# Giving the small matmuls of a recurrent attention kernel one tile shape each, and evacuating the end of a segment in halves

## The chip, the core and the metric

The kernel runs on one core of a Trainium2 chip. The metric is device time in microseconds, from the start of the program to its end. Five engines matter here: TensorE (in the profile PE for matmuls and PEld for weight loads), VectorE (DVE), ScalarE (ACT), GpSimd (POOL) and SyncE (SP), which issues most DMAs. Each engine works off its own queue in order; semaphores tie the queues together. A matmul takes a stationary operand (the loaded weights, `lhsT`) and a moving operand (`rhs`); a tile shape such as 32*128 or 128*64 in the profile means that the matmul uses so many rows and columns of the array. Results land in PSUM, from where VectorE or ScalarE copy them to SBUF. Such a copy is called an evacuation here.

## The reference

Two attention layers are computed from separate inputs and set side by side in the output. Part A is a sliding local attention; the change does not touch it. Part B is a recurrent attention with memory, and nearly all of the time is spent there:

```python
for s in range(n_seg):                       # 64 segments of 32 tokens
    xs = x[:, s * seg_len:(s + 1) * seg_len, :].copy()
    h = jnp.concatenate([mem, xs], axis=1)   # 8 memory rows + 32 tokens = 40
    q = jnp.einsum('btd,dhe->bhte', h, Wq)   # 640 -> 32 heads of 192
    k = jnp.einsum('btd,dhe->bhte', h, Wk)
    v = jnp.einsum('btd,dhe->bhte', h, Wv)
    scores = jnp.einsum('bhqe,bhke->bhqk', q, k) * scale
    scores = jnp.where(mask[None, None], scores, -1000000000.0)
    p = _softmax(scores, axis=-1)
    o = jnp.einsum('bhqk,bhke->bhqe', p, v)
    o = jnp.einsum('bhte,hed->btd', o, Wo)
    mem = o[:, :M, :].copy()                 # the next segment's memory
    outs.append(o[:, M:, :])
```

The segments form a chain: the first 8 output rows of one are the memory of the next. Matrices are bfloat16.

## The kernel before, in words

Part B works through 64 segments. In each, the 32 heads are taken as 4 groups (`g`) of 8 heads; a group's projection is 8 x 192 = 1536 columns wide. `project32` computes one projection of one group for 32 rows of the input: four matmuls of tile 128*32 stand side by side in the array, so the result `acc` has 128 partitions (4 column blocks of 32 tokens) and 384 columns (two heads of 192). A segment's 40 rows are 32 main rows and 8 late ones. The late rows of four segments are projected together, in 32 rows at once, only when a group is due (`RENEW`), and are kept until their segment comes (in `Lb` buffers for Q and K, in `LV` for V).

For Q and K, `to_sb` evacuates `acc` into `sb`; `turn` transposes the three 128-column chunks of `sb` into the PSUM tile `pt` (partitions = positions within two heads, free = chunk, block, token); `spread` copies it into `QT` or `KT`. The two heads of a block take 384 positions, so chunk 0 belongs to the first head, chunk 2 to the second, and the middle chunk is half and half. `turn_late` does the same for the late rows, into `QT`/`KT` or into `Lb`; POOL copies from `Lb` later (L488).

`scores(g)` computes all 8 heads' scores into one PSUM tile `Sps`: for each head one matmul over a whole chunk (128 rows, tile 128*64) and one over half of the middle chunk (64 rows, tile 64*64). `softmax` is a chain on VectorE and ScalarE; `put_p` writes the normalized result into `P`; `turn_p` transposes `P` with two 128*128 transposes and evacuates it into `PT`. `mix(g)` multiplies `PT` with V: per group 16 matmuls of tile 32*128 (whole chunks) and 16 of tile 32*64 (halves of the middle chunk) into four PSUM tiles `OTps`, which are evacuated into `OT`. `project_out` accumulates `OT` times `Wo` into `Y` with tiles of 128*64.

At the end of a segment `Y` is evacuated into `row` (`Ysb`, L643, one ScalarE copy of 320 columns), `memory_rows` transposes the 8 memory rows into the next segment's input `HX`, and the late Q of one group, which was projected meanwhile, is evacuated into `sb` and turned.

What sets the order: TensorE's order is the order of the calls in `segment`, written out by hand (`manual_schedule` for PE alone). The order on VectorE, ScalarE, POOL and SP is made by the framework's scheduler. `evacuate` alternates between ScalarE and VectorE by a count over all its calls, so that one more or one fewer call moves all later ones to the other engine:

```python
    def evacuate(dst, src):
        copies["n"] += 1
        (nc.scalar.copy if copies["n"] % 2 else nc.vector.tensor_copy)(dst, src)
```

PSUM is held by three pools: 3 buffers for `acc`, 4 for everything small (`ps_x`: `pt`, `Sps`, `OTps`), 1 for `Y`. Weights that do not fit in SBUF are streamed in every segment by SP through 5 slots (`ws`, tile name `t` in the profile, read from `wcopy_k`, `wcopy_v` and `wcopy_o`): 23 units a segment.

Of the kernel before, what the change touches and what calls it, by code (L numbers as in the profile page):

```python
# [271 lines left out]
def part_b(ctx, tc, B_x, B_mem0, B_Wq, B_Wk, B_Wv, B_Wo, out, ident, n_seg, pre, nbuf, mid):  # L272
# [139 lines left out]
    free = [cpool.tile([128, 12, M], BF16, name=f"Lb{i}") for i in range(BLOCKS)]  # L412
# [35 lines left out]
    def to_sb(p):  # L448
        sb = qk_sb.tile([128, 384], BF16, tag="sb", name="sb")
        evacuate(sb[:], p[:])  # L450
        return sb

    def turn(sb):
        pt = ps_x.tile([128, 3, 4, 32], FP32, tag="x")
        for c in range(3):
            nc.tensor.matmul(pt[:, c], lhsT=sb[:, 128 * c:128 * c + 128], rhs=ident, start=True, stop=True)  # L456
        return pt

    def spread(dst, src):
        evacuate(dst.rearrange("p (j c) n -> p c j n", c=3), src)  # L460

    def tokens(t):
        return t[:, 0:12 * L].rearrange("p (a n) -> p a n", n=L)

    def turn_late(sb, m, g, s, start):

        pt = turn(sb)
        T = tokens(QT if m == "q" else KT)
        for t in range(start, next_start(m, g, start)):
            if t == s:  # L470
                dst = T[:, :, 32:L]
            else:
                late[m, g, t] = free.pop(0)
                dst = late[m, g, t][:]
            spread(dst, pt[:, :, :, M * (t % 4):M * (t % 4) + M])

    def project_qk(s, m, g):
        T = QT if m == "q" else KT
        renew = s == 0 or f"{m}{g}" in RENEW[s % 4]
        Xs = [ahead(s), main(s)] if renew else [main(s)]  # L480
        sbs = [to_sb(p) for p in project32(Xs, m, g)]

        def turns():
            if renew:
                turn_late(sbs[0], m, g, s, s)
            else:
                b = late.pop((m, g, s))
                nc.gpsimd.tensor_copy(tokens(T)[:, :, 32:L], b[:])  # L488
                free.append(b)
            pt = turn(sbs[-1])  # L490
            spread(tokens(T)[:, :, 0:32], pt[:])

        return turns

    def values(s, g):
        renew = s == 0 or f"v{g}" in RENEW[s % 4]
        ps = project32([ahead(s), main(s)] if renew else [main(s)], "v", g)
        if renew:
            evacuate(LV[g][:], ps[0][:])
        Vst = one.tile([128, 384], BF16, tag="Vst")  # L500
        evacuate(Vst[:], ps[-1][:])
        return Vst

    def scores(g):
        KTt = tokens(KT)
        Sps = ps_x.tile([128, 4, L], FP32, tag="x")
        plist = []
        for a in range(4):
            plist += [(False, 0, a, 0, 3 * a, 128), (True, 0, a, 0, 3 * a + 1, 64),
                      (True, 64, a, 1, 3 * a + 1, 128), (False, 0, a, 1, 3 * a + 2, 128)]  # L510
        plist.sort()
        seen = set()
        last = {p[3]: n for n, p in enumerate(plist)}
        for n, (_, lo, a, g2, cc, hi) in enumerate(plist):
            nc.tensor.matmul(Sps[64 * g2:64 * g2 + 64, a, :], lhsT=QT[lo:hi, L * cc:L * cc + 64], rhs=KTt[lo:hi, cc, :],  # L515
                             start=(g2 not in seen), stop=(n == last[g2]), tile_position=(lo, 64 * g2))
            seen.add(g2)
        return Sps

    def softmax(Sps):  # L520
# [19 lines left out]
            nc.vector.tensor_tensor(out=P[:, k, :, at:at + hi - lo], in0=t1[:, :, lo:hi],  # L540
                                    in1=sm[:].unsqueeze(2).to_broadcast([128, 4, hi - lo]), op=ALU.mult)

    def turn_p():

        pt = ps_x.tile([128, 2, 128], BF16, tag="x")
        for late in range(2):
            nc.tensor.transpose(pt[:, late, :], P[:, late].rearrange("p a n -> p (a n)"), ident)  # L547
# [4 lines left out]
    def mix(g, PT, Vst):  # L552

        ps = [ps_x.tile([128, 3, L], FP32, tag="x", name=f"OTps{a}") for a in range(4)]
        for wide in (True, False):
            for late, V in enumerate((Vst, LV[g])):
                for half in range(2):
                    for a in range(4):
                        if wide:
                            dst, e0, e1, col = ps[a][:, 2 * half, :], 256 * half, 256 * half + 128, 0  # L560
                        else:
                            dst, e0, e1 = ps[a][64 * half:64 * half + 64, 1, :], 128 + 64 * half, 192 + 64 * half
                            col = 64 * half
                        nc.tensor.matmul(dst, lhsT=V[32 * a:32 * a + 32, e0:e1], rhs=PT[32 * a:32 * a + 32, late, half, :],  # L564
                                         start=(wide and late == 0 and half == 0), stop=(not wide and late == 1),
                                         tile_position=(32 * a, col))
# [14 lines left out]

    def memory_rows(s, Ysb):
        pt = ps_x.tile([128, 5, M], FP32, tag="x")
        for dc in range(5):
            for gv in range(2):
                c0, c1 = max(128 * dc, 320 * gv), min(128 * dc + 128, 320 * gv + 320)
                if c0 < c1:
                    lo = c0 - 128 * dc
                    nc.tensor.matmul(pt[lo:lo + c1 - c0, dc, :], lhsT=Ysb[:, c0 - 320 * gv:c1 - 320 * gv],
                                     rhs=ident[:, 64 * gv:64 * gv + M], start=True, stop=True,  # L590
                                     tile_position=(0, lo))
        nc.vector.tensor_copy(HXs[(s + 1) % 2][:, :, 0:M], pt[:])

    def segment(s):
        last = s + 1 == n_seg
        load_x(s + 1)
        tq, tk, V, PT = {}, {}, {}, {}
# [10 lines left out]
        V[0] = values(s, 0)  # L608
# [5 lines left out]
        mix(0, PT[0], V[0])  # L614
        V[1] = values(s, 1)
# [7 lines left out]
        mix(1, PT[1], V[1])  # L623
        V[2] = values(s, 2)
# [6 lines left out]
        mix(2, PT[2], V[2])  # L631
        V[3] = values(s, 3)
        project_out(Y, 2, range(0, 4))
        PT[3] = turn_p()
        project_out(Y, 2, range(4, 6))
        mix(3, PT[3], V[3])
# [6 lines left out]
        nc.scalar.copy(Ysb, Y[:])  # L643
# [84 lines left out]
```

## Time and profile before

| | |
|---|---|
| time, median of 3 runs | 2028.95 us (2024.3 to 2034.06) |
| profiled execution, device time | 2024.66 us |
| profiled execution, span of its instructions | 2022.8 us |
| busy: PE / PEld | 1945.4 / 1243.6 us |
| busy: DVE / ACT / POOL | 1128.3 / 725.6 / 193.6 us |
| instructions | 97144, of them 42512 matmuls and as many weight loads |
| granted TensorE clock, mean | 0.994 |
| HBM read and written | 576.85 MB and 18.87 MB, 295 GB/s over the span |

The span is 1.9 us shorter than the device time; what lies around it is small. The profile's rows give a start in microseconds, a length from the first start to the last end of a merged group, and in brackets how long the engine was idle before and what ended that. A matmul's length holds its way through the array, so matmuls that follow each other overlap in the records; what a matmul costs on TensorE is seen from start to start, not from its length.

### The profile page before, as it was taken

What the parts mean: (1) busy time and instruction counts of PE and PEld (TensorE: products, weight loads), DVE (VectorE), ACT (ScalarE), POOL (GpSimd) and SP (SyncE); (2) the same over time, 40 slices, a digit from 0 to 9 for tenths busy, and PEclk for the clock granted to TensorE, in tenths of its full rate; (3) what the DMA queues carried; (4) which work ended last, traced back from release to release, by engine and by line L of the source; (5) the groups of instructions that cost most, each with busy time, mean ns of one, the idle gap of its engine ahead of it and who ended that gap; (6) DMA issues with size and microseconds to landing.
All of it is one profiled execution on the core that took longest, in us unless ns stands there. A gap on an engine that the chain in (4) does not pass through costs nothing.

```text
span 2022.8 us, 97144 instructions
## 1 busy us (share of the span) xinstructions
PE 1945.4 (96%) x42512; PEld 1243.6 (61%) x42512; DVE 1128.3 (56%) x3622; ACT 725.6 (36%) x2126; POOL 193.6 (10%) x674
## 2 busy tenths in 40 slices
PE   7989999999999999999999999999999999999998
PEld 4656666666666666666666666666666665666665
DVE  5875555555555455555555555555555554555554
ACT  3543333333333333333333333333333333333333
POOL 2000000110001101001001001101001001110110
PEclk9999999999999999999999999999999999999999
DMA  9927999999899999999999989999899988989997
GB/s 343 311 76 269 311 300 305 301 302 307 290 305 304 299 288 312 302 304 303 303 299 297 308 292 311 305 303 299 296 298 303 298 304 284 303 293 300 305 302 257
DMA packets 270123, 596.29 MB, mean 295 GB/s; under 512 B 61065, under 2 KB 72841, under 8 KB 269385
## 3 DMA queue, kind: packets, MB, share of 16 engines
q1 hardware_dynamic: 264770, 585.97, 87.9%
q8 instruction: 333, 5.46, 1.1%
q0 software_dynamic: 4928, 4.11, 0.6%
q14 instruction: 92, 0.75, 0.1%
HBM read 576.85 MB, written 18.87 MB: 295 GB/s over the span
## 4 chain that ended last, share of the span: by engine, by line
PE 71%; DMA 19%; DVE 6%; ACT 1%; issue 1%; SPq 1%; POOL 0%; DVEq 0%; POOLq 0%; ACTq 0%
PE acc L443 33%; PE Y L578 18%; DMA t<-wcopy_k 8%; DMA t<-wcopy_o 6%; PE pt L456 6%; PE Sps L515 4%; PE OTps L564 4%; PE pq L95 2%; PE pt L547 2%; DVE sb L423 2%; DMA out_dram<-row 2%; DMA t<-wcopy_v 1%; PE po L161 1%; DMA wcopy_o<-in_B_Wo_dram 1%; PE py L172 1%
## 5 line engine op out<-in xcount | busy, mean ns | idle before, releaser
L443 PEld LDWEIGHTS <-HX 128*32 128x32 bf16 x19380 | 462.7, 96 | 274.3 <-issue 46.5
L578 PEld LDWEIGHTS <-OT 128*64 128x64 bf16 x6144 | 316.8, 109 | 131.0 <-ACT OT L423 20.0
L578 PE MATMUL Y<-wres_o,OT 128*64 128x320 bf16 x3584 | 344.3, 302 | 2.2
L443 PE MATMUL acc<-wres_q,HX 128*32 128x384 bf16 x6460 | 332.6, 328 | 0.5 <-ACT sb L423 0.2
L443 PE MATMUL acc<-t,HX 128*32 128x384 bf16 x4200 | 309.1, 328 | 12.9 <-DMA t<-wcopy_k 10.1
L578 PE MATMUL Y<-t,OT 128*64 128x320 bf16 x2560 | 277.7, 303 | 10.0 <-DMA t<-wcopy_o 9.2
L423 DVE CAST sb<-acc 128x384 bf16<-128x384 f32 x322 | 178.8, 556 | 186.6 <-PE acc L443 171.3
L443 PE MATMUL acc<-wres_v,HX 128*32 128x384 bf16 x4844 | 276.5, 328 | 0.1
L528 ACT ACTIVATE t<-t 128x160 f32<-128x160 f32 x256 | 86.1, 336 | 439.4 <-DVE t L527 439.4
L443 PE MATMUL acc<-wres_k,HX 128*32 128x384 bf16 x3876 | 224.8, 327 | 0.3 <-issue 0.3
L522 DVE SCALAR_TENSOR_TENSOR t<-Sps,mask 128x160 f32<-128x160 f32 x256 | 82.8, 323 | 214.6 <-PE Sps L515 186.6
L423 ACT CAST sb<-acc 128x384 bf16<-128x384 f32 x324 | 153.6, 474 | 125.1 <-PE acc L443 123.5
L456 PE MATMUL pt<-ident,sb 128*128 128x128 bf16 x1938 | 179.4, 221 | 6.9 <-DVE sb L423 1.7
L423 DVE CAST OT<-OTps 128x120 bf16<-128x120 f32 x512 | 125.5, 271 | 97.4 <-PE OTps L564 96.8
L488 POOL COPY QT<-Lb 128x96 bf16<-128x96 bf16 x252 | 67.4, 267 | 1112.0 <-PE Sps L515 955.2
L456 PEld LDWEIGHTS <-sb 128*128 128x128 bf16 x1938 | 110.2, 97 | 82.3 <-issue 32.3
L515 PEld LDWEIGHTS <-QT 128*64 128x64 bf16 (+1 forms) x4096 | 118.9, 109 | 55.1 <-issue 40.5
L423 ACT CAST OT<-OTps 128x120 bf16<-128x120 f32 x512 | 106.0, 258 | 110.7 <-PE OTps L564 110.4
L515 PE MATMUL Sps<-KT,QT 128*64 128x40 bf16 (+1 forms) x4096 | 137.0, 188 | 2.2 <-DVE KT L423 1.0
L530 DVE TENSOR_REDUCE sm<-t 128x4 f32<-128x160 f32 x256 | 81.8, 320 | 78.7 <-ACT t L528 78.7
L564 PEld LDWEIGHTS <-Vst 32*128 32x128 bf16 (+1 forms) x4096 | 62.2, 97 | 82.3 <-issue 60.5
L564 PE MATMUL OTps<-PT,Vst 32*128 32x40 bf16 (+1 forms) x4096 | 109.7, 192 | 0.0
(75 smaller groups left out, 1916.0 us busy)
## 6 DMA issues: line engine op xcount, KB each, us to landing
t<-wcopy_o SPq DMA_DIRECT2D x640, 320.0 KB, 4.3
t<-wcopy_k SPq DMA_DIRECT2D x512, 384.0 KB, 4.8
t<-wcopy_v SPq DMA_DIRECT2D x320, 384.0 KB, 4.8
wres_q<-in_B_Wq_dram SPq DMA_DIRECT2D x20, 384.0 KB, 7.7
wres_v<-in_B_Wv_dram SPq DMA_DIRECT2D x15, 384.0 KB, 7.8
wres_k<-in_B_Wk_dram SPq DMA_DIRECT2D x12, 384.0 KB, 7.7
wres_o<-in_B_Wo_dram SPq DMA_DIRECT2D x14, 320.0 KB, 6.7
wcopy_o<-in_B_Wo_dram SPq DMA_DIRECT2D x10, 320.0 KB, 8.1
```

The source lines that it names most:

```text
L95: nc.tensor.matmul(pq[32 * d:32 * d + 32], lhsT=wcol[:, k, t, 4 * c + d, :], rhs=xTs[s][:, k, :], start=(k == 0), stop=(k == 4), tile_posi ...
L423: (nc.scalar.copy if copies["n"] % 2 else nc.vector.tensor_copy)(dst, src)
L443: nc.tensor.matmul(ps[n][32 * j:32 * j + 32, :], lhsT=X[:, dc, :], rhs=w[:, 384 * j:384 * j + 384], start=(dc == 0), stop=(dc == 4), tile_ ...
L456: nc.tensor.matmul(pt[:, c], lhsT=sb[:, 128 * c:128 * c + 128], rhs=ident, start=True, stop=True)
L488: nc.gpsimd.tensor_copy(tokens(T)[:, :, 32:L], b[:])
L515: nc.tensor.matmul(Sps[64 * g2:64 * g2 + 64, a, :], lhsT=QT[lo:hi, L * cc:L * cc + 64], rhs=KTt[lo:hi, cc, :], start=(g2 not in seen), sto ...
L522: nc.vector.scalar_tensor_tensor(out=t1[:], in0=Sps[:], scalar=scale, in1=mask[:].unsqueeze(1).to_broadcast([128, 4, L]), op0=ALU.mult, op ...
L528: nc.scalar.activation(t1[:], t1[:], ACTF.Exp)
L530: nc.vector.tensor_reduce(out=sm[:], in_=t1[:], axis=AX.X, op=ALU.add)
L547: nc.tensor.transpose(pt[:, late, :], P[:, late].rearrange("p a n -> p (a n)"), ident)
L564: nc.tensor.matmul(dst, lhsT=V[32 * a:32 * a + 32, e0:e1], rhs=PT[32 * a:32 * a + 32, late, half, :], start=(wide and late == 0 and half = ...
L578: nc.tensor.matmul(Y[64 * gv:64 * gv + 64, :], lhsT=OT[:, L * c:L * c + 64], rhs=w[:, n:n + 320], start=(i == 0 and r == 0), stop=(i == 23 ...
```

## The change

All edits are in part B.

- **V with zeros inside.** `Vst` and `LV` grow from 384 to 448 columns, with 64 zero columns between the two heads. Each half of the middle chunk can then be taken as a whole 128-column chunk whose other half is zero. `mix` issues 32 matmuls of tile 32*128, as many as before in all, and none of 32*64.
- **K's middle chunk twice.** `KT` holds four chunks for each block: the first head's, the middle one with its lower half zero, the second head's, and the middle one with its upper half zero. `scores` issues 16 matmuls of tile 128*64, as many as before in all, and none of 64*64. K can no longer be copied from `pt` in one piece: `fill` takes one copy of two chunks (256 columns for the main rows) and two copies of 64 partitions (128 columns each), in place of one copy of 384. The same holds for the late rows, also for POOL's copies from `Lb`.
- **Transposes of the last group's P.** `turn_p(2)` does, for group 3 alone, four matmuls of tile 128*64 against the identity into float32 in place of two transposes of 128*128.
- **End of a segment.** `Y` into `row` and the late Q into `sb` are each copied in two halves, the first by ScalarE and the second by VectorE. `memory_rows` takes its middle chunk, which needs tile 128*64, first.

```diff
-    KT = cpool.tile([128, 12 * L], BF16, name="KT")
+    KT = cpool.tile([128, 4, 4, L], BF16, name="KT")
...
-    LV = [cpool.tile([128, 384], BF16, name=f"Lv{g}") for g in range(GROUPS)]
+    VW = 448
+    LV = [cpool.tile([128, VW], BF16, name=f"Lv{g}") for g in range(GROUPS)]
+    Vst = cpool.tile([128, VW], BF16, name="Vst")
     nc.gpsimd.memset(P[:], 0.0)
+    nc.gpsimd.memset(KT[:], 0.0)
...
+    for t in LV + [Vst]:
+        nc.gpsimd.memset(t[:, 192:256], 0.0)
...
+    def halves(dst, src, n):
+        nc.scalar.copy(dst[:, 0:n], src[:, 0:n])
+        nc.vector.tensor_copy(dst[:, n:], src[:, n:])
...
+    def fill(copy, m, n0, n1, src):
+
+        if m == "q":
+            copy(tokens(QT)[:, :, :, n0:n1].rearrange("p j c n -> p c j n"), src)
+            return
+        copy(KT[:, :, 0:3:2, n0:n1].rearrange("p j c n -> p c j n"), src[:, 0:3:2])
+        copy(KT[0:64, :, 1, n0:n1], src[0:64, 1])
+        copy(KT[64:128, :, 3, n0:n1], src[64:128, 1])
...
+        for n in range(8):
+            a, part = n // 2, n % 2
+            for g2 in range(2):
+                at = L * (3 * a + g2 + part)
+                nc.tensor.matmul(Sps[64 * g2:64 * g2 + 64, a, :], lhsT=QT[:, at:at + 64],
+                                 rhs=KT[:, a, ((0, 1), (3, 2))[g2][part], :], start=(n == 0), stop=(n == 7),
+                                 tile_position=(0, 64 * g2))
...
+            for h in range(2):
+                nc.tensor.matmul(pt[64 * h:64 * h + 64, late, :], lhsT=src[:, 64 * h:64 * h + 64], rhs=ident,
+                                 start=True, stop=True, tile_position=(0, 64 * h))
...
+        plan = [(late, half, k, col) for late in range(2) for half in range(2)
+                for k, col in (((0, 0), (1, 128)), ((2, 320), (1, 192)))[half]]
+        for n, (late, half, k, col) in enumerate(plan):
+            V = LV[g] if late else Vst
+            for a in range(4):
+                nc.tensor.matmul(ps[a][:, k, :], lhsT=V[32 * a:32 * a + 32, col:col + 128],
+                                 rhs=PT[32 * a:32 * a + 32, late, half, :],
+                                 start=(n == 0), stop=(n == len(plan) - 1), tile_position=(32 * a, 0))
...
-        for dc in range(5):
+        for dc in (2, 0, 1, 3, 4):
...
-        PT[3] = turn_p()
+        PT[3] = turn_p(2)
...
-        nc.scalar.copy(Ysb, Y[:])
+        halves(Ysb, Y[:], 160)
         if not last:
             project32([ahead(s + 1)], "q", gl, range(3, 5), ql)
-            sb = to_sb(ql[0])
+            sb = qk_sb.tile([128, 384], BF16, tag="sb", name="sb")
+            halves(sb[:], ql[0][:], 192)
```

More of the change, by code (lines that the diff above doesn't have):

```diff
@@ L497, in values @@
         ps = project32([ahead(s), main(s)] if renew else [main(s)], "v", g)
[L498 to L502, printed above, removed]
+        for t, p in ((LV[g], ps[0]), (Vst, ps[-1]))[0 if renew else 1:]:
+            v = t[:].rearrange("p (n e) -> p n e", e=64)
+            w = bass.AP(v.tensor, v.offset, [v.ap[0], [256, 2], [1, 192]])
+            evacuate(w, p[:].rearrange("p (h e) -> p h e", h=2))
     def scores(g):
-        KTt = tokens(KT)
         Sps = ps_x.tile([128, 4, L], FP32, tag="x")
[L507 to L517, printed above, removed]
+        for n in range(8):
[5 more added lines that the diff above has]
+                                 tile_position=(0, 64 * g2))
         return Sps
@@ L541, in put_p, with turn_p @@
                                     in1=sm[:].unsqueeze(2).to_broadcast([128, 4, hi - lo]), op=ALU.mult)
-    def turn_p():
-        pt = ps_x.tile([128, 2, 128], BF16, tag="x")
+    def turn_p(split=1):
+        pt = ps_x.tile([128, 2, 128], FP32 if split > 1 else BF16, tag="x")
         for late in range(2):
-            nc.tensor.transpose(pt[:, late, :], P[:, late].rearrange("p a n -> p (a n)"), ident)
+            src = P[:, late].rearrange("p a n -> p (a n)")
+            if split == 1:
+                nc.tensor.transpose(pt[:, late, :], src, ident)
+                continue
+            for h in range(2):
+                nc.tensor.matmul(pt[64 * h:64 * h + 64, late, :], lhsT=src[:, 64 * h:64 * h + 64], rhs=ident,
+                                 start=True, stop=True, tile_position=(0, 64 * h))
         PT = one.tile([128, 2, 2, L], BF16, tag="PT")
@@ L550, in turn_p, with mix @@
         return PT
-    def mix(g, PT, Vst):
+    def mix(g, PT):
         ps = [ps_x.tile([128, 3, L], FP32, tag="x", name=f"OTps{a}") for a in range(4)]
[L555 to L566, printed above, removed]
+        plan = [(late, half, k, col) for late in range(2) for half in range(2)
[6 more added lines that the diff above has]
+                                 start=(n == 0), stop=(n == len(plan) - 1), tile_position=(32 * a, 0))
         for a in range(4):
@@ L607, in segment @@
         tq[2] = project_qk(s, "q", 2)
-        V[0] = values(s, 0)
+        values(s, 0)
         soft = softmax(scores(1))
@@ L613, in segment @@
         tk[2] = project_qk(s, "k", 2)
-        mix(0, PT[0], V[0])
-        V[1] = values(s, 1)
+        mix(0, PT[0])
+        values(s, 1)
         tk[2]()
@@ L622, in segment @@
         tk[3] = project_qk(s, "k", 3)
-        mix(1, PT[1], V[1])
-        V[2] = values(s, 2)
+        mix(1, PT[1])
+        values(s, 2)
         tq[3]()
```

27 lines of the change are left out of this document (11 added, 16 removed).

## The prediction, made before the changed kernel ran

> **What bounds the kernel now.** I read the page's head and its chain first, then a sum over the steady stretch, then the waits, then the timeline around each edit.
>
> ```profile
> span 2022.8 us, 97144 instructions
> ```
> ```profile
> PE 71%; DMA 19%; DVE 6%; ACT 1%; issue 1%; SPq 1%; POOL 0%; DVEq 0%; POOLq 0%; ACTq 0%
> ```
> ```profile
> 200.00:2000.00 1800.00, 1753.56 (x39782) 1122.67 (x39778) 986.25 (x3426) 628.04 (x1920) 176.98 (x629) 1.00 0.92 301
> ```
> ```profile
> PE acc L443 <- DMA t<-wcopy_k: 10.1, 32, 0.9
> ```
>
> In the steady stretch PE is busy for 1753.56 of 1800 us at clock 1.00, and VectorE for 986.25. The DMA share is 0.92, but the longest sum of waits of a matmul for a streamed unit is 10.1 us. So TensorE's order sets the time. A stall in it counts, and so does a saving, until a streamed unit is late.
>
> **Mix.** Four mixes in each of 64 segments. One of them:
>
> ```profile
> 1025.30 0.22 PE L564 MATMUL OTps<-PT,Vst 32*128 32x40 bf16 x8
> 1025.36 0.21 PE L564 MATMUL OTps<-PT,Lv 32*128 32x40 bf16 x8
> 1025.50 0.23 PE L564 MATMUL OTps<-PT,Vst 32*64 32x40 bf16 x8
> 1025.55 0.20 PE L564 MATMUL OTps<-PT,Lv 32*64 32x40 bf16 x8
> 1025.68 0.35 PE L443 MATMUL acc<-wres_v,HX 128*32 128x384 bf16 x4
> ```
> ```profile
> L564 PE MATMUL OTps<-PT,Lv 32*128 32x40 bf16 x2048 | 53.6, 174 | 0.0
> ```
>
> The last wide matmul starts at 1025.36 + 0.21 - 0.174 = 1025.40, the first narrow one at 1025.50: the change of shape costs 0.10 us, in which eight matmuls start elsewhere (0.05 to 0.06). The whole lasts 0.38. Afterwards 32 wide ones take 0.10 for the first sixteen, 0.10 to 0.12 for the others, and 0.11 for the way out (as from narrow: 1025.50 to 1025.68, less 0.07). That is 0.30 to 0.32, so 0.06 to 0.08 saved; I take 0.08, since the second eight started in 0.04. Four: 0.33 a segment.
>
> **Scores.**
>
> ```profile
> 1020.51 0.30 PE L515 MATMUL Sps<-KT,QT 128*64 128x40 bf16 x8
> ```
> ```profile
> 1020.75 0.31 PE L515 MATMUL Sps<-KT,QT 64*64 64x40 bf16 x8
> ```
> ```profile
> 1020.99 0.68 PE L456 MATMUL pt<-ident,sb 128*128 128x128 bf16 x9
> ```
> ```profile
> 1006.61 0.52 PE L515 MATMUL Sps<-KT,QT 128*64 128x40 bf16 x16
> 1007.06 0.46 PE L578 MATMUL Y<-wres_o,OT 128*64 128x320 bf16 x4
> ```
>
> Eight wide ones and the change of shape last 0.24, eight narrow ones and the next change 0.24. Wide ones start in pairs; the last starts at 1020.51 + 0.30 - 0.186 (its length in this window) = 1020.63, so eight take 0.12. Sixteen of one shape take 0.25, plus 0.11 for the way out: 0.36 against 0.48, 0.12 saved in groups 0 to 2. Group 3 stands between matmuls of Y with the same tile 128*64, so both changes go: 0.45 becomes about 0.25, 0.20 saved. Together 0.55 a segment. New is that two pairs running add to the same 40 columns. Matmuls of Y add to the same 320 columns without a gap (four in 0.27 us below), so I take nothing for it; a pair that waited for the whole length of the one before (0.19) would cost 8 x 0.15 a group, the far end.
>
> **Transposes of the last P.**
>
> ```profile
> 1009.61 0.44 PE L578 MATMUL Y<-t,OT 128*64 128x320 bf16 x4
> 1009.88 0.44 PE L578 MATMUL Y<-wres_o,OT 128*64 128x320 bf16 x4
> 1010.25 0.28 PE L547 MATMUL pt<-ident,P 128*128 128x128 bf16 x2
> 1010.47 0.33 PE L578 MATMUL Y<-wres_o,OT 128*64 128x320 bf16 x2
> ```
>
> Y starts a pair every 0.135 us, so its last starts at 1010.02, and Y goes on 0.45 later. With one shape that is 0.135 plus two pairs of 128 columns (0.055 each by the same rate): 0.24, so 0.21 saved. Here a rule can be weighed: two shape changes go, and by the rows each is dear by some 0.1. The Trainium skill, TensorEngine Tiling (Array Packing), Key Properties, says that a change of tiling mode drains the array while a change of tile does not; no price is given there, and the gaps above show about 0.1.
>
> Savings: 0.33 + 0.55 + 0.21 = **1.09 us a segment, 70 us**.
>
> **Copies that take turns.** `fill` copies K from one PSUM tile in three copies, alternating between ScalarE and VectorE, and `halves` splits two evacuations. In the changed order each later copy of such a set waits for a semaphore of the other engine. The trace has this already, in the `Lb` copies from one `pt`:
>
> ```profile
> 1015.71 0.26 DVE L423 CAST Lb<-pt 128x96 bf16<-128x96 f32 x1 [0.25 <-PE pt L456]
> 1016.05 0.24 ACT L423 CAST Lb<-pt 128x96 bf16<-128x96 f32 x1 [0.85 <-DVE Lb L423]
> 1016.39 0.26 DVE L423 CAST Lb<-pt 128x96 bf16<-128x96 f32 x1 [0.43 <-ACT Lb L423]
> ```
> ```profile
> L423 DVE CAST KT<-pt 128x384 bf16<-128x384 f32 x113 | 62.1, 549 | 0.0
> ```
> ```profile
> L164 ACT CAST ao<-po 128x256 bf16<-128x256 f32 x8 | 3.0, 372 | 2.6 <-PE po L161 2.6
> ```
>
> They run one after the other with 0.08 to 0.10 between. Lengths between these rows: on ScalarE 256 columns 0.37, 128 columns 0.27, 160 columns 0.29, 192 columns 0.32; on VectorE 0.42, 0.29, 0.32 and 0.35. So K lies ready 0.37 + 0.10 + 0.29 + 0.09 + 0.27 = 1.12 us after its first copy starts, against 0.48 to 0.55 now: 0.6 later. The Trainium skill, PSUM — Partial Sum Buffer, Terms, says that two engines must not touch one bank in one quadrant at once, and that different quadrants of a bank may be used side by side. The halves of `Y` and `sb` fall under the first. The two K copies of 64 partitions lie in different quadrants, and if they ran side by side K would be 0.36 earlier; the semaphores in the changed order speak against it.
>
> **K's wait.** How much of the 0.6 is hidden, by kind of segment:
>
> ```profile
> 1220.28 0.71 DVE L423 CAST KT<-pt 128x96 bf16<-128x96 f32 x2
> ```
> ```profile
> 1221.05 0.55 PE L515 MATMUL Sps<-KT,QT 128*64 128x40 bf16 x16
> ```
> ```profile
> 1247.48 0.55 DVE L423 CAST KT<-pt 128x384 bf16<-128x384 f32 x1
> 1249.06 0.55 PE L515 MATMUL Sps<-KT,QT 128*64 128x40 bf16 x16
> ```
> ```profile
> 1275.85 0.48 ACT L423 CAST KT<-pt 128x384 bf16<-128x384 f32 x1
> ```
> ```profile
> 1276.67 0.55 PE L515 MATMUL Sps<-KT,QT 128*64 128x40 bf16 x16
> ```
> ```profile
> 1033.09 0.48 ACT L423 CAST KT<-pt 128x384 bf16<-128x384 f32 x1
> ```
> ```profile
> 1034.15 0.52 PE L515 MATMUL Sps<-KT,QT 128*64 128x40 bf16 x16
> ```
>
> The first three are `scores(0)`. Where K's group 0 is renewed (1220) K is ready 0.06 before use, just in time, and the renewed rows' three copies come in front: I take 0.41. Where group 1 is (1247), 1.03 is to spare: nothing. In the two other kinds (1275) it is 0.34, of which 0.05 is the hand-over itself, and the first copy starts some 0.07 later in its queue: 0.6 + 0.07 - 0.29, so 0.37 each. Mean 0.29 a segment. `scores(3)` (1033) has 0.58 to spare, and P's copy (0.23 on VectorE) stands between K's: 0.6 + 0.15 - 0.58 + 0.05 = 0.22. `scores(2)` follows 24 matmuls of Y and loses nothing; `scores(1)` loses something only where its K is renewed, mean 0.07. Bounds: nothing to 0.6 for `scores(0)` and `scores(3)`.
>
> **P's wait.**
>
> ```profile
> PEld L547 <- DVE P L540: 13.9, 42, 0.9
> ```
>
> VectorE computes the softmax in order, and between its steps stand copies of Q, K and `sb`. TensorE waits for P already, above all before a segment's first transposes of it, up to 0.9 at a time. The new alternation puts two K copies more into that chain in two kinds (0.3 to 0.4 later there, while TensorE comes 0.23 earlier by two scores), and in a third takes a Q copy and an `sb` copy (0.55 each) out for K copies of 0.42 and 0.29. I take 0.15 as the mean, between -0.3 and +0.5.
>
> **End of a segment.**
>
> ```profile
> 1014.27 0.42 ACT L643 CAST row<-Y 128x320 bf16<-128x320 f32 x1 [2.12 <-PE Y L578]
> 1014.73 0.48 ACT L423 CAST sb<-acc 128x384 bf16<-128x384 f32 x1
> ```
> ```profile
> 1015.26 0.20 DVE L592 CAST HX<-pt 128x40 bf16<-128x40 f32 x1 [3.08 <-PE pt L589]
> 1015.26 0.34 PE L456 MATMUL pt<-ident,sb 128*128 128x128 bf16 x3
> 1015.53 0.51 PE L443 MATMUL acc<-wres_q,HX 128*32 128x384 bf16 x8
> ```
>
> Now `row` is ready at 1014.69 and `sb` at 1015.21, and the next segment begins at 1015.53. In halves: `row` 0.29 + 0.09 + 0.32, ready at 1014.97; the first half of `sb` 1014.73 to 1015.05, the second 1015.14 to 1015.49. The turn starts at 1015.55 and the next segment 0.27 later, 1015.82: +0.29 here. Over all I take 0.25, since where VectorE copies the whole `sb` now (0.55) the end is later already. The saved shape change in `memory_rows` (0.07) lies under the wait for `sb`. Side by side the halves would have given about -0.13.
>
> ```profile
> DVE t L522 <- DMA out_dram<-row: 14.6, 12, 1.9
> ```
>
> `row` lies in the softmax's tile `t`, so the next segment's first softmax waits for POOL's output DMAs, which now start 0.28 later. The first scores come 0.25 + 0.29 later themselves, so I add nothing; the DMAs have no one else behind them.
>
> **Streamed units.** o's last units stand behind mix(3) and P's transposes, 0.29 less time to land; K's first units gain 0.25 behind the longer end. I take 0.05, between 0 and 0.3. POOL's extra K copies and memsets and the V copies of unchanged size lie in idle time (POOL is busy for 177 of 1800 us).
>
> **Sum.** 0.29 + 0.07 + 0.22 + 0.15 + 0.25 + 0.05 = 1.03 lost, 1.09 saved: 0.06 x 64 = 4 us faster. Against the execution's 2024.66 that is 2021; the median of the runs lies 4.3 higher, so **2025**, no measurable change (0.5%, 10 us, is about what a measurement of this kernel can tell from none).
>
> **The rivals.**
> - *K's copies are hidden* (24%): the scores lose next to nothing, by 1.03 to spare in one kind and 24 matmuls of Y before `scores(2)`. 0.58 x 64 = 37 us: 1988. Against it: 0.06, 0.34 and 0.58 elsewhere.
> - *The softmax chain pays in every segment* (34%): three K copies that take turns across two in-order queues hold up the exponential on ScalarE and the sums on VectorE. If the exponential comes 0.3 later in every kind, P's 0.15 becomes 0.48 and `scores(1)` loses 0.28 in all: 0.54 x 64 = 35, **2060**, slower. It decides from 0.25 of delay on. For it: P is late in most segments already.
> - *Quadrants side by side* (3%): the two small K copies overlap, and K is 0.29 + 0.09 earlier at both waits of scores: 0.29 and 0.22 shrink to about 0.05 together, 0.46 x 64 = 29: 1996. The Trainium skill, PSUM — Partial Sum Buffer, Terms, allows it; the order of semaphores does not.
> - *Adding to the same columns* (3%): a pair waits 0.03 for the one before: 8 x 0.03 x 256 = 61, 2086.
>
> **How the numbers follow.** 36% for the balance, with its own range of 2005 to 2045 (terms 0.3 off together). Over 2039 lie the second and the fourth rival and 2 of the 36: 39% slower. Under 2019 the first, the third and 7 of the 36: 34% faster. 27% within 0.5%. The range of eight in ten reaches from 1980 to 2075.
>
> **What would show it.** Mix rows of 32*128 alone, 0.31 from first to next; scores of 128*64 alone, 0.36, and no gap at Y in group 3; two idle stretches of PE or PEld before Sps with KT as releaser, 0.2 to 0.4 each; `row` and `sb` halves one after the other and some 1.55 in place of 1.26 us from the start of `row`'s copy to the next segment's first matmul. It is wrong if KT never releases a scores, if the halves overlap, or if matmuls wait for streamed units for over 0.3 us a segment more.

## The result, and the profile after

| | before | changed |
|---|---|---|
| median of 20 runs each, us | 2027.26 (2018.12 to 2035.58) | 2017.05 (2007.98 to 2028.15) |
| ratio, 95% interval | | 0.9952 [0.9938, 0.9966] |
| the profiled execution, us (its span) | 2024.66 (2022.8) | 2021.62 (2019.8) |

The change makes the kernel some 10 us faster, 0.48%, just inside the half per cent that the prediction named as no measurable change. The interval excludes 1, so a small gain is real. The profiled execution of the changed kernel lies 4.6 us above the median of its runs, so single rows are read from it, and the sum is read from the medians.

The chain of the changed kernel's page, and the steady stretch (PE, PEld, DVE, ACT, POOL busy; PE clock; DMA share; GB/s):

```profile
PE 55%; DMA 24%; DVE 15%; issue 3%; ACT 3%; SPq 0%; POOL 0%; DVEq 0%; ACTq 0%; POOLq 0%
```
```profile
200.00:2000.00 1800.00, 1709.53 (x39985) 1092.14 (x39981) 1084.96 (x3843) 678.90 (x2269) 241.51 (x1007) 1.00 0.92 302
```

TensorE is busy 44 us less than before (1753.56), VectorE 99 us more. The busy time saved is real, but most of it has become idle time of TensorE: the chain was 71% PE and now is 55%, with DMA up from 19% to 24% and VectorE from 6% to 15%. The timeline of the changed kernel at the places that the prediction named (start, length, engine, line, operation, in brackets the idle time before it and what ended that; rows between that bear on nothing here are left out):

```profile
1099.89 1.17 DVE L428 CAST KT<-pt 128x64 bf16<-128x64 f32 x4
1100.51 0.21 PE L521 MATMUL Sps<-KT,QT 128*64 128x40 bf16 x1
1101.11 0.37 PE L521 MATMUL Sps<-KT,QT 128*64 128x40 bf16 x13 [0.40 <-DVE KT L428]
...
1113.95 0.38 ACT L428 CAST KT<-pt 128x256 bf16<-128x256 f32 x1
1114.37 0.28 DVE L428 CAST KT<-pt 64x128 bf16<-64x128 f32 x1
...
1114.68 0.26 ACT L428 CAST KT<-pt 64x128 bf16<-64x128 f32 x1 [0.35 <-DVE KT L428]
1115.07 0.41 PE L521 MATMUL Sps<-KT,QT 128*64 128x40 bf16 x16
1115.32 0.44 PE L586 MATMUL Y<-wres_o,OT 128*64 128x320 bf16 x4
...
1118.52 0.28 PE L558 MATMUL pt<-ident,P 128*64 128x128 bf16 x4
1118.63 0.44 PE L586 MATMUL Y<-wres_o,OT 128*64 128x320 bf16 x4
...
1119.35 0.27 PE L572 MATMUL OTps<-PT,Vst 32*128 32x40 bf16 x16
1119.46 0.26 PE L572 MATMUL OTps<-PT,Lv 32*128 32x40 bf16 x16
1119.66 0.67 PE L448 MATMUL acc<-wres_q,HX 128*32 128x384 bf16 x12
...
1122.12 0.29 ACT L459 CAST row<-Y 128x160 bf16<-128x160 f32 x1 [1.84 <-PE Y L586]
1122.44 0.33 DVE L460 CAST row<-Y 128x160 bf16<-128x160 f32 x1 [2.13 <-ACT row L459]
1122.57 0.32 ACT L459 CAST sb<-acc 128x192 bf16<-128x192 f32 x1 [0.16 <-PE acc L448]
1122.92 0.36 DVE L460 CAST sb<-acc 128x192 bf16<-128x192 f32 x1 [0.15 <-ACT sb L459]
1123.07 0.56 PE L465 MATMUL pt<-ident,sb 128*128 128x128 bf16 x3
...
1123.55 1.00 PE L448 MATMUL acc<-wres_q,HX 128*32 128x384 bf16 x20
...
1157.17 0.26 ACT L428 CAST KT<-pt 64x128 bf16<-64x128 f32 x1 [0.35 <-DVE KT L428]
1157.26 0.62 PE L521 MATMUL Sps<-KT,QT 128*64 128x40 bf16 x16
```

One by one:
- *Mix* (1119.35): 0.31 us to the next `acc` here, 0.30 as a rule, against 0.38.
- *Last P* (1118.52): its four matmuls hand over to Y after 0.11 us.
- *Scores in group 3* (1115.07): Y goes on 0.25 us later, against 0.45. K was ready at 1114.68 + 0.26 = 1114.94, 0.13 before use: no wait.
- *Scores in group 0*: where K's group 0 is renewed (1100.51) the first goes and 13 wait until 1101.11 (two records are missing). Where neither group 0 nor 1 is (1157.26), the sixteen take 0.62 in place of 0.41.
- *The end*: the halves do take turns, but the second starts 0.03 us after the first has ended, not 0.09, and the first turn starts at 1123.07, before the second half of `sb` is there (1122.92 + 0.36 = 1123.28). From `row` to the next segment's first matmul it is 1123.55 - 1122.12 = 1.43 us, against 1.26.

What the sums of waits of the changed kernel say (line waited for: us in all, times, longest), and three rows of the kernel before that had no part in the prediction:

```profile
PEld L448 <- issue: 50.6, 156, 1.1
...
PEld L586 <- issue: 32.2, 60, 1.7
...
PEld L555 <- DVE P L546: 21.6, 70, 0.4
PE Y L586 <- DMA t<-wcopy_o: 20.3, 41, 1.5
```
```profile
PEld L443 <- issue: 46.5, 140, 1.1
...
PEld L578 <- issue: 19.7, 44, 0.9
...
PE Y L578 <- DMA t<-wcopy_o: 9.2, 23, 0.8
```

The wait of Y's matmuls for streamed units of o has doubled, from 9.2 to 20.3 us. Idle time ahead of weight loads that the profile puts down to nothing it shows ("issue") has grown as well, from 19.7 to 32.2 us for Y and from 46.5 to 50.6 for `acc`. Between them the stream looks like the place where the saving went, and the experiments were made to test that.

### The profile page after: what moved, and what is told of

It is laid out like the page before. It is cut to its first block, busy times and chain, and to the rows that moved or that the text cites. A ratio compares the mean times of both kernels' runs of the same rounds, so it can differ in the third digit from the quotient of the medians.

```text
span 2019.8 us, 98671 instructions
## 1 busy us (share of the span) xinstructions
PE 1899.0 (94%) x42640; PEld 1210.0 (60%) x42640; DVE 1226.9 (61%) x4041; ACT 777.0 (38%) x2480; POOL 259.3 (13%) x1058
## 4 chain that ended last, share of the span: by engine, by line
PE 55%; DMA 24%; DVE 15%; issue 3%; ACT 3%; SPq 0%; POOL 0%; DVEq 0%; ACTq 0%; POOLq 0%
PE acc L448 24%; PE Y L586 14%; DMA t<-wcopy_o 10%; DMA t<-wcopy_k 8%; PE pt L465 4%; PE pq L95 3%; PE Sps L521 3%; DMA out_dram<-row 3%; DMA t<-wcopy_v 2%; PE OTps L572 2%; DVE sb L428 2%; PE po L161 1%; DVE P L546 1%; DVE QT L428 1%; DVE sm L536 1%
## 5 line engine op out<-in xcount | busy, mean ns | idle before, releaser
L448 PEld LDWEIGHTS <-HX 128*32 128x32 bf16 x19380 | 466.2, 96 | 283.4 <-issue 50.6
L586 PE MATMUL Y<-t,OT 128*64 128x320 bf16 x2560 | 280.9, 303 | 21.9 <-DMA t<-wcopy_o 20.3
L428 DVE CAST sb<-acc 128x384 bf16<-128x384 f32 x291 | 160.9, 553 | 103.6 <-PE acc L448 87.1
L465 PE MATMUL pt<-ident,sb 128*128 128x128 bf16 x1938 | 190.5, 221 | 9.8 <-DVE sb L428 4.2
L428 ACT CAST sb<-acc 128x384 bf16<-128x384 f32 x292 | 138.8, 475 | 143.3 <-PE acc L448 136.3
L428 ACT CAST KT<-pt 64x128 bf16<-64x128 f32 (+3 forms) x517 | 139.3, 277 | 112.9 <-DVE KT L428 72.3
L428 DVE CAST KT<-pt 64x128 bf16<-64x128 f32 (+2 forms) x452 | 134.2, 300 | 31.1 <-ACT KT L428 23.0
L478 POOL COPY KT<-Lb 64x32 bf16<-64x32 bf16 x189 | 41.4, 219 | 825.1 <-PE Sps L521 825.1
L521 PEld LDWEIGHTS <-QT 128*64 128x64 bf16 x4096 | 100.3, 112 | 59.4 <-issue 50.3
L428 ACT CAST Vst<-acc 128x384 bf16<-128x384 f32 x205 | 98.7, 481 | 95.6 <-PE acc L448 92.0
L521 PE MATMUL Sps<-KT,QT 128*64 128x40 bf16 x4096 | 117.6, 187 | 9.2 <-DVE KT L428 6.2
```

Source lines behind the costliest of these rows:

```text
L448: nc.tensor.matmul(ps[n][32 * j:32 * j + 32, :], lhsT=X[:, dc, :], rhs=w[:, 384 * j:384 * j + 384], start=(dc == 0), stop=(dc == 4), tile_ ...
L478: copy(KT[64:128, :, 3, n0:n1], src[64:128, 1])
L521: nc.tensor.matmul(Sps[64 * g2:64 * g2 + 64, a, :], lhsT=QT[:, at:at + 64], rhs=KT[:, a, ((0, 1), (3, 2))[g2][part], :], start=(n == 0), s ...
L586: nc.tensor.matmul(Y[64 * gv:64 * gv + 64, :], lhsT=OT[:, L * c:L * c + 64], rhs=w[:, n:n + 320], start=(i == 0 and r == 0), stop=(i == 23 ...
```

## The experiments

Times are compared as ratios to the kernel before, run on the same chip beside each of them; 0.001 is 2.0 us. An interval reaches 0.0014 to 0.0041 to each side, mostly some 0.0018 (3.7 us). A difference of two ratios is then good to some 5 us.

**One part undone at a time.** Four kernels, each the changed one with one part as before:

```diff
-        halves(Ysb, Y[:], 160)
+        nc.scalar.copy(Ysb, Y[:])
...
-            halves(sb[:], ql[0][:], 192)
+            nc.scalar.copy(sb[:], ql[0][:])
```

> The end of a segment with whole copies on ScalarE again, everything else as changed. Theory (the halves take turns and cost time): the stretch from the last Y matmul to the next segment grew from 1.635 to 1.775 us, 0.14 a segment; it falls back to about 1.63, 64 x 0.14 = 9 us faster than the changed kernel, ratio to before about 0.991. Rival (the streamed units set the pace there: K's first units of the next segment come no earlier): the wait moves to acc<-wcopy_k and the time stays within 3 us of the changed kernel, ratio 0.994 to 0.997. Second rival (the halves did help, since the first turn starts before the second half is there): slower, ratio above 0.998.

```diff
-        copy(KT[:, :, 0:3:2, n0:n1].rearrange("p j c n -> p c j n"), src[:, 0:3:2])
-        copy(KT[0:64, :, 1, n0:n1], src[0:64, 1])
-        copy(KT[64:128, :, 3, n0:n1], src[64:128, 1])
+        copy(KT[:, :, 0:3, n0:n1].rearrange("p j c n -> p c j n"), src)
```

with `scores` as before:

> K and the scores as before (one copy of K, two tile shapes), everything else as changed. Theory (what the four scores gain by one shape is more than what they wait for K): the medians by place say -0.115, -0.19, -0.09 and +0.125 us, together 0.27 a segment; undone, the time rises by 64 x 0.27 = 17 us, ratio to before about 1.003. Rival (three K copies in turns also hold up the softmax, P and the order of the other copies, which the stretch of the scores alone does not show): undone, the time changes by less than 5 us or falls, ratio 0.990 to 0.997, and the waits of matmuls for P shrink.

```diff
-            v = t[:].rearrange("p (n e) -> p n e", e=64)
-            w = bass.AP(v.tensor, v.offset, [v.ap[0], [256, 2], [1, 192]])
-            evacuate(w, p[:].rearrange("p (h e) -> p h e", h=2))
+            evacuate(t[:, 0:384], p[:])
```

with `mix` as before:

> V and the mixes as before (wide and narrow tiles), everything else as changed. Theory (the mix's saving of 0.085 us each reaches the end in full): 4 x 0.085 x 64 = 22 us slower, ratio to before about 1.006. Rival (part of it was given back, because Y's matmuls then wait for streamed units of o: their waits rose from 22.8 to 37.4 us in all): undone, Y's waits fall by some 10 us and the time rises by 8 to 14 us only, ratio 0.999 to 1.002.

```diff
-        PT[3] = turn_p(2)
+        PT[3] = turn_p()
```

> The last P of a segment is turned by whole transposes of 128*128 as before, everything else as changed. Theory (two shape changes less are worth 0.20 us a segment): undone, 64 x 0.20 = 13 us slower, ratio to before about 1.0015. Rival (the saving is given back at once: the Y matmuls of o3.1 and o3.2 behind it wait for their streamed unit instead): the time stays within 5 us of the changed kernel, and the wait Y<-wcopy_o shrinks by as much.

| undone | ratio to before, 95% | us against the changed kernel (ratio less 0.9952, x 2035) |
|---|---|---|
| halves at the end | 0.9925 [0.9905, 0.9944] | -5.5 |
| K and scores | 0.9991 [0.9973, 1.0009] | +7.9 |
| V and mixes | 0.9983 [0.9966, 1.0000] | +6.3 |
| last P | 0.9960 [0.9944, 0.9976] | +1.6 |

Each difference is good to some 5 us. K's and V's parts help, and the halves cost, 5.5 us where 9 were expected; the last P's part can't be told from nothing. The parts sum to 7.9 + 6.3 + 1.6 - 5.5 = 10.3 us, where the whole change brought 9.8, but with four such margins that closeness is no proof that nothing else acts. But V's part and the last P's bring 6 and 2 us where their rows say 22 and 13: the rivals of those two expectations were nearer, and V's fell even short of its own 8 to 14. The sign that V's rival named didn't show either: with V as before Y's matmuls wait 22.5 us for units of o, not some 10 less than the 20.3 of the changed kernel. With the last P as before it is 18.1. For K 8 us lies between both expectations (17, and under 5), and the wait of the weight loads for P shrinks as the rival said, from 21.6 us to

```profile
PEld L557 <- DVE P L548: 14.5, 44, 0.6
```
With the whole tail, the timeline of a segment's end reads:

```profile
1130.82 0.43 ACT L651 CAST row<-Y 128x320 bf16<-128x320 f32 x1 [1.83 <-PE Y L586]
...
1132.07 0.51 PE L448 MATMUL acc<-wres_q,HX 128*32 128x384 bf16 x8
```

From `row` to the next segment 1.25 us again, 0.18 less than with halves; 64 x 0.18 = 11.5 us by place, of which 5.5 (to some 5) arrive.

**A lighter stream.** If the stream takes the rest back, the change must be worth more without it. In both kernels 7 of the 23 streamed units of a segment are not loaded:

```diff
     def get_unit(u):
+        u = {("k", 1, 4): ("k", 1, 1), ("v", 1, 1): ("v", 1, 0), ("o", 4, 0): ("o", 3, 0), ("o", 11, 0): ("o", 10, 0),
+             ("v", 3, 2): ("v", 3, 1), ("o", 17, 0): ("o", 16, 0), ("o", 22, 0): ("o", 21, 0)}.get(u, u)
```

> The kernel before with 7 of the 23 streamed units of a segment not loaded: a resident neighbour stands in for them, so these products use other weights and 30% of the stream is left out. It sets the mark for the next run. Both theories: matmuls of the kernel before wait for streamed units for some 23 us in all, so 10 to 25 us faster than before, ratio 0.988 to 0.995.

> The changed kernel with the same 7 of 23 streamed units not loaded. Theory (what TensorE saves is given back to the stream: undoing V's part or the last P's part moved the time by 6 and 2 us where the rows by place say 22 and 13): without that cover the sum by place, 0.31 mix + 0.27 scores + 0.19 last P - 0.14 end - 0.12 turns = 0.5 us a segment, reaches the end, so 30 us faster than the kernel before with the same units left out, ratio to it 0.983 to 0.987. Rival (the savings are lost in PSUM, copies and the softmax chain, not in the stream): the difference stays at 10 us, ratio to it 0.994 to 0.997.

Kernel before with the lighter stream: 1979.37 us, ratio 0.9732 [0.9707, 0.9757]. Changed kernel with it: 1951.48, 0.9593 [0.9568, 0.9619]. The steady stretch of the two, the kernel before first:

```profile
200.00:1900.00 1700.00, 1682.52 (x38587) 1083.89 (x38585) 955.45 (x3321) 609.53 (x1861) 171.38 (x608) 1.00 0.71 220
```
```profile
200.00:1900.00 1700.00, 1647.94 (x39259) 1060.91 (x39257) 1063.18 (x3770) 666.03 (x2229) 235.63 (x987) 1.00 0.72 223
```

With the DMA share at 0.71 and 0.72 in place of 0.92, the change brings 1979.4 - 1951.5 = 28 us, 1.4%, as the theory said, and not 10. So the full stream takes some 18 of 28 us back. The first expectation was missed by far: the kernel before gains 55 us (2.7%), not 10 to 25. Named waits for streamed units (10.1 us for k, 9.2 for o, 3.5 in smaller rows: 22.8) were less than half of what the stream cost. Another part stood under "issue", ahead of weight loads. In the kernel before with the lighter stream these two rows are

```profile
PEld L445 <- issue: 19.0, 70, 0.5
...
PEld L580 <- issue: 5.1, 16, 0.3
```

where they were 46.5 for `acc` and 19.7 for Y: 42 us less together. (One stall can stand in a row of PE and in one of PEld, so these and the 22.8 are not to be added up to the 55.)

In both kernels with the lighter stream, no wait for a streamed unit is left in the sums. Their rows are so regular that the change can be read place by place, as the mean time from the first matmul of one group to the first of the next, over segments 4 to 62:

| place | us a segment, before to changed |
|---|---|
| four mixes | -0.32 |
| `scores(0)`: 0.48 to 0.94 (K's group 0 renewed), 0.36 (group 1), 0.58 and 0.56 (the others) | +0.13 |
| `scores(1)` | -0.10 |
| `scores(2)` | -0.12 |
| `scores(3)` and Y behind it | -0.20 |
| last P and Y around it | -0.20 |
| end of the segment | +0.14 |
| turns of Q, K and P | +0.10 |
| `acc` behind the mixes and Y, waiting for OT | +0.16 |
| others | -0.01 |
| sum | -0.42, x 64 = 27 us |

The same places in the two profiled executions with the full stream (3 us apart) sum to -0.04 a segment only. Two of them make up 0.30 of the 0.37 between the two pairs. The first projections of a segment grow by 0.15 with the full stream and by nothing with the lighter one, and the last matmuls of Y by 0.17 against 0.02. Both take streamed units.

**Where V's saving goes even so.** Two more kernels with the lighter stream, the whole tail and V as before:

> The changed kernel with whole copies at the end of a segment and the same 7 of 23 streamed units not loaded. Theory (the halves cost 0.14 us a segment, and the full stream gave part of the gain back): without that cover 64 x 0.14 = 9 us less than the changed kernel with the lighter stream, 1942 against 1951, ratio 0.9548 against 0.9593. Rival (the 5 us measured with the full stream are all there is): 0.957.

> The changed kernel with V and the mixes as before and the same 7 of 23 streamed units not loaded. Theory (the mixes' 0.34 us a segment is real, and the full stream took three quarters of it back): 19 to 22 us more than the changed kernel with the lighter stream, 1970 to 1974, ratio 0.969 to 0.970. Rival (the saving by place is given back in PSUM and copies and not in the stream): 6 us more, 0.962.

Whole tail: 1940.3 us, 11 less than the changed kernel's 1951.5, ratio 0.9527 [0.9491, 0.9562]. (The two lighter kernels here ran on another chip than the two above; the kernel before took 2035.4 us there and 2036.1 beside those.) By place it is 0.17 a segment, 11 us: here the whole of it arrives. V as before: 1964.2, ratio 0.9644 [0.9603, 0.9685], 12.7 us more, between the two expectations. The mixes are 0.33 longer by place, but 0.16 comes back elsewhere, above all between mix(2) and Y. First the changed kernel, then V as before, both with the lighter stream, from `scores(3)` on:

```profile
1088.68 0.41 PE L523 MATMUL Sps<-KT,QT 128*64 128x40 bf16 x16
...
1089.58 0.27 PE L574 MATMUL OTps<-PT,Vst 32*128 32x40 bf16 x16
...
1090.36 0.34 ACT L536 ACTIVATE t<-t 128x160 f32<-128x160 f32 x1 [1.79 <-DVE t L535]
1090.72 0.42 ACT L430 CAST OT<-OTps 128x120 bf16<-128x120 f32 x2
...
1091.03 0.41 PEld L588 LDWEIGHTS <-OT 128*64 128x64 bf16 x8 [0.54 <-ACT OT L430]
```
```profile
1094.38 0.41 PE L521 MATMUL Sps<-KT,QT 128*64 128x40 bf16 x16
...
1095.28 0.22 PE L576 MATMUL OTps<-PT,Vst 32*128 32x40 bf16 x8
...
1096.05 0.34 ACT L534 ACTIVATE t<-t 128x160 f32<-128x160 f32 x1 [1.79 <-DVE t L533]
1096.41 0.42 ACT L430 CAST OT<-OTps 128x120 bf16<-128x120 f32 x2
...
1096.72 0.41 PEld L590 LDWEIGHTS <-OT 128*64 128x64 bf16 x8 [0.45 <-ACT OT L430]
```

From `scores(3)` to Y's first weight load it is 2.35 and 2.34 us, whatever the mix takes. ScalarE works in order: its copies of OT stand behind the exponential of `scores(3)`, that waits for VectorE, and Y waits for OT. A shorter mix(2) only waits longer there (0.54 against 0.45). So that mix's 0.09 is lost in such segments before the stream sees anything.

**K's copies on one engine.** With the whole tail, each fill takes one engine for its three copies:

```diff
+        if copy is evacuate:
+            copies["n"] += 1
+            copy = nc.scalar.copy if copies["n"] % 2 else nc.vector.tensor_copy
         copy(KT[:, :, 0:3:2, n0:n1].rearrange("p j c n -> p c j n"), src[:, 0:3:2])
```

> Whole copies at the end of a segment, and K's three copies of one fill all on one engine (ScalarE and VectorE alternate by fill), else as changed. Theory (every hand-over between the engines costs 0.08 to 0.10 us and lies in scores(0)'s wait for K): five hand-overs go where K's group 0 is renewed, two in two other kinds, so scores(0) comes 0.1 to 0.4 earlier there, 0.15 a segment; 10 us less than with the whole copies alone where the stream lets it through, 3 to 5 us where it gives half of it back: ratio to before 0.988 to 0.991. Rival (the length of the copies and the place in the queue decide, not the hand-over): within 3 us of the whole copies alone, ratio 0.991 to 0.994.

2035.17 us, ratio 1.0007 [0.9991, 1.0022]: 17 us slower than the whole tail alone, which neither expectation had. Where a fill stands alone its copies go as hoped for:

```profile
1117.61 0.37 ACT L479 CAST KT<-pt 128x256 bf16<-128x256 f32 x1 [1.12 <-PE pt L465]
1117.87 0.26 ACT L480 CAST KT<-pt 64x128 bf16<-64x128 f32 x1
1118.15 0.26 ACT L481 CAST KT<-pt 64x128 bf16<-64x128 f32 x1
```

K is there after 0.80 us (1118.41 - 1117.61) where taking turns it needs 0.99 (1114.94 - 1113.95), and in the two kinds with neither group 0 nor 1 renewed `scores(0)` shrinks by 0.15 and 0.12. But the next group of turns is 0.22 and 0.19 longer there, and where K's group 1 is renewed `scores(1)` grows by 0.26 and the turns after it by 0.36. The waits of turns for `sb` show it, with one engine first and then with the whole tail alone:

```profile
PEld L465 <- DVE sb L428: 27.1, 67, 1.1
```
```profile
PEld L465 <- DVE sb L428: 15.4, 34, 1.1
```

Those rows point to the three K copies in a row, which keep the next `sb` waiting in an engine that works in order.

By place, 9 of the 17 us have another reason. Where K's group 0 is renewed, `scores(0)` begins 0.43 us later on the mean and lasts 0.14 longer, 0.14 a segment over the four kinds. K has two fills there, and between them stand three copies of `Lb`, which take the alternation on as well. So both fills fall to VectorE, in every such segment, and the first matmul waits for its fourth K copy:

```profile
1114.96 0.21 DVE L479 CAST KT<-pt 128x64 bf16<-128x64 f32 x1
...
1115.50 0.42 DVE L479 CAST KT<-pt 128x256 bf16<-128x256 f32 x1
...
1115.98 0.18 PE L524 MATMUL Sps<-KT,QT 128*64 128x40 bf16 x1 [0.34 <-DVE KT L479]
```

So this run doesn't price one engine against hand-overs alone; a count that gave the two fills to different engines was not tried.

**The zeros in Q.** With the whole tail, Q's middle chunk is held twice and K is one copy:

```diff
+        if m == "k":
+            copy(KT[:, :, :, n0:n1].rearrange("p j c n -> p c j n"), src)
+            return
+        Q = tokens(QT)
+        copy(Q[:, :, 0:3:2, n0:n1].rearrange("p j c n -> p c j n"), src[:, 0:3:2])
+        copy(Q[0:64, :, 1, n0:n1], src[0:64, 1])
+        copy(Q[64:128, :, 3, n0:n1], src[64:128, 1])
...
```

> Zeros in Q instead of K: Q's middle chunk is held twice with zeros and K is one copy again, so the scores keep their one shape; whole copies at the end of a segment. Theory (scores(0) wait for the last of K's three copies, and Q is turned 0.4 us before K): Q's copies end while K is turned, the waits of 0.57 and 0.20 us at scores(0) shrink by 0.2 to 0.4 and 0.1 to 0.2; 0.15 to 0.2 us a segment by place, of which the stream takes half back: 5 to 7 us less than with K's zeros and the whole tail, ratio to before 0.988 to 0.991. Rival (the place in the in-order queues decides: Q's three copies stand ahead of K's one and it comes as late): scores(0) wait as before, ratio 0.991 to 0.995.

2031.48 us, ratio 0.9979 [0.9961, 0.9997], 11 us slower than the whole tail with K's zeros: outside both expectations. Where K's group 0 is renewed `scores(0)` falls from 0.94 to 0.45, as the theory said; in the two other kinds it stays (0.51 and 0.52), as the rival said. A new wait decides, at mix(0):

```profile
1117.76 0.20 PE L572 MATMUL OTps<-PT,Vst 32*128 32x40 bf16 x3
1117.99 0.29 DVE L427 CAST QT<-pt 64x128 bf16<-64x128 f32 x1
1118.34 0.25 PE L572 MATMUL OTps<-PT,Vst 32*128 32x40 bf16 x13 [0.38 <-DVE QT L427]
...
1118.62 0.35 PE L447 MATMUL acc<-wres_v,HX 128*32 128x384 bf16 x4
```

A mix takes four PSUM tiles, all that this pool has, and one still holds the turned Q until its third copy has ended at 1117.99 + 0.29 = 1118.28. The mix lasts 0.86 instead of 0.30; over all kinds 0.37 a segment.

**The alternation.** One call more, `copies["n"] += 1`, at the end of each segment, once with the zeros in Q and once in the changed kernel (where it gives each engine back the calls that it had before the change, but for K's pieces):

> The same with the alternation of ScalarE and VectorE set on by one call at the end of each segment, so every later copy of a segment changes its engine. Theory (which engine takes which copy matters only by where the long copies fall, and that evens out over four kinds of segment): within 4 us of zeros_in_q. Rival (the chain from scores to P is held up by particular copies): 8 us or more apart from it, one way or the other, with the difference in the waits of the transposes for P or of the scores for K.

> The changed kernel with one call more in the alternation at the end of a segment, so that ScalarE and VectorE take the same calls as in the kernel before. Theory (the prediction's: the flipped alternation makes P 0.15 us a segment later): 0.15 x 64 = 10 us less by place and half of it in time, ratio to before 0.990 to 0.994. Rival (the three K copies and not the flip hold up the chain): within 3 us of the changed kernel, 0.994 to 0.997, or slower.

0.9983 [0.9967, 1.0000] against 0.9979, and 0.9956 [0.9939, 0.9972] against 0.9952: no difference in either pair. The wait for P in the changed kernel with the call added is no shorter than the 21.6 us without it:

```profile
PEld L555 <- DVE P L546: 24.4, 74, 1.0
```

So the flip of the alternation isn't what makes P late; with K as before the same wait was 14.5, so K's part of the change is. Whether its copies do it, or its shorter scores that bring TensorE there earlier, was not parted.

## Why the prediction came out as it did

The forecast, no measurable change, holds at 9.8 us faster, at the edge of what it allowed. The number was in part luck, because two errors of the sum cancel: the path on the engines gained about four times what the sum had, and the stream took most of that back.

- *Mix, 0.33.* Measured 0.32. *Last P, 0.21.* 0.20. *Scores, 0.12 each and 0.20 in group 3.* 0.12 where nothing waits, 0.20 in group 3. Everything that was read off as a price of a change of shape holds; each change of shape less is worth 0.09 us (mix) to 0.12 (scores in groups 0 to 2). The Trainium skill, TensorEngine Tiling (Array Packing), Key Properties, says that a change of tiling mode drains the array. These prices fit it; that the array drains, no row here shows.
- *Adding to the same columns, nothing.* It holds: sixteen scores of one shape take 0.25 us between matmuls of Y.
- *Hand-overs of 0.08 to 0.10 us.* This was taken from copies of `Lb`. In the halves and in K's copies the second engine starts 0.03 to 0.04 us after the first. With the first turn starting before `sb` is whole, the end costs 0.14 where 0.25 was forecast.
- *Scores waiting for K, 0.29, 0.07 and 0.22.* `scores(0)` waits 0.25 us on the mean (+0.13 net of 0.12 saved), 0.58 in the kind with group 0 renewed, nothing with group 1, 0.22 and 0.20 in the others: the kinds were right. `scores(1)` waits some 0.02. `scores(3)` has its saving in full: in the rows above K's copies end 0.13 before use, where the sum let them cost 0.22. Most of that term was never there, and it is the largest error among the waits.
- *P's wait, 0.15.* The size is about right (0.10 in the turns of Q, K and P), the cause only in part. The flip of the alternation does nothing that these runs can tell; K's part of the change does.
- *OT.* Not in the sum: 0.16, of which 0.07 lies behind mix(2), where copies of OT behind the exponential hold Y, 0.07 behind mix(3) and 0.02 in Y, whose cause no row above shows. The first is the softmax rival at one place; as a whole, a delay that pays everywhere, that rival didn't come about.
- *Streamed units, 0.05.* This is the step that failed. The whole change brings 28 us with the lighter stream and 10 with the full one, so the stream takes 18 / 64 = 0.28 a segment, near the upper end of the 0 to 0.3 that was allowed. The waits that bear a streamed unit's name rose from 22.8 to 37.4 us in all, 0.23 a segment. The prediction read 10.1 us of named waits and took the cover for ample, though the chain that it shows had 19% DMA. The kernel before lost 55 us already to the 7 units that the lighter stream leaves out, much of it as idle time ahead of weight loads that bears no name.

Without the stream the sum would have read 1.09 - 0.98 = 0.11 a segment, 7 us, against 28 measured; with it, 4 against 10. Of the other rivals, K's copies stay hidden for `scores(2)` and `scores(3)`, nearly so for `scores(1)`, and not for `scores(0)`; quadrants side by side didn't come about, since the small K copies take turns (1114.37 and 1114.68 above).

The changed kernel with whole copies at the end is faster than the kernel before: 2019.67 us beside 2035.46, ratio 0.9925 [0.9905, 0.9944]. Its interval still touches that of the changed kernel; with the lighter stream the same edit gives 11 us, outside the scatter there (1937.95 to 1941.03 against 1948.65 to 1953.01 us).

What stays open: whether another choice of streamed units would let more of the 28 us through was not tried. Nor was it tested what in the stream binds, the DMA engines, the five slots or the order of the loads: leaving units out eases all three.

## What to carry to other kernels

A saving on the bounding engine is worth what the next limit leaves of it. Where the DMA share is 0.92, take a part of the stream out of both versions before trusting a sum by place: the difference between the two pairs (28 and 10 us here) is what the stream takes. Look for waits on a stream under idle time without a name ahead of weight loads, too. And before an evacuation is cut into pieces, ask what stands behind the pieces in both queues, to which engine each falls, and which buffer they keep: rearranging K's and Q's pieces to save waits cost 17 and 11 us here.

## What was not expected of the hardware

- A hand-over between ScalarE and VectorE has two sizes here: 0.03 to 0.04 us in the halves and K's copies, 0.08 to 0.10 in the copies of `Lb`. Why is open.
- Three copies of one PSUM tile in a row on ScalarE take less time than their lengths: they start 0.26 and 0.28 apart, though the first is listed with 0.37, so 0.80 us for 0.89.
- With a DMA share of 0.92 the runs scatter by 0.6% (17 runs of the kernel before, 2027.15 to 2039.86 us, beside the lighter ones); at 0.71 and 0.72 the four or five runs of each of the four lighter kernels lie within 0.1 to 0.23% (1978.32 to 1980.22 us for the lighter kernel before).
